# Sliding-window attention into a squared-ReLU MLP: two tiles loaded plainly, masks first, w_in ahead of w_out, global copies on VectorE, and the kT and xT evacuations on ScalarE

## Chip, cores, metric

One core of a Trainium2 chip. The metric is the device time of one execution in microseconds (us), the median of several. TensorE is called PE, VectorE DVE, ScalarE ACT, GpSimd POOL. An evacuation is a copy out of the PSUM tile into which PE has written; B4 is unit B of tile 4 (the units are explained below). "Cold" is PE at a lower granted clock. Profile line numbers (L189) belong to each kernel's own file, so one statement has different numbers before and after.

## The reference, cut

```python
# q, k, v: (4, 8, 768, 64) fp32; n_global = 8, n_local = 96
scores = q @ k.T / sqrt(64)
keep   = (column < 8) | (0 <= row - column < 96)
scores = where(keep, scores - slope[h] * dist, -1e9)   # ALiBi bias
attn   = softmax(scores) @ v                           # -> x (3072, 512)
out    = relu(x @ w_in) ** 2 @ w_out                   # w_in (512, 2048), w_out (2048, 512)
```

## The kernel before: what the argument touches

Attention is cut into 24 tiles of 128 rows, six a batch element, each in units A to F. The MLP is cut into 96 steps: 12 blocks of two tiles, by 8 slices of d_ff. "Stage 1" of a step makes hT, hr and hs; "stage 2" adds into acc and, at a block's end, copies acc out. A loop deals units between stages.

```python
def unit_a(j):                       # q and k of tile j transposed into ONE psum tile
    tr = ps_tr.tile([P, 2 * NPAIR, P], BF16, name="tr", tag="tr")    # bufs=1
    ... 4 transposes of q, 4 of k (PE) ...
    nc.vector.tensor_copy(z[:D, :, 0, :], tr[:D, :NPAIR, :])         # qz
    nc.vector.tensor_copy(z[D:, :, 1, :], tr[D:, :NPAIR, :])         # qz
    nc.vector.tensor_copy(kT[j], tr[:, NPAIR:, :])                   # kT

def globals_k(j):                    # after the scores of tile j
    nc.gpsimd.tensor_copy(kT[j][:, :, :n_global], g[:, :, :n_global])

# B, C (scores): matmuls into sc (bufs=1); esc = exp(sc) on ACT; at = esc * E on DVE
# D, E (values): matmuls into po (bufs=1); rs, x on DVE
# F: transposes of x into a tile of the same single "tr" buffer; xT copied out

def stage1(g):   # 8 matmuls -> hT (bufs=2); hr = relu(hT) on ACT; hs = hr*hr on DVE
def stage2(g):   # 4 matmuls -> acc (two psum tiles, bufs=1 each)
    if s == NSTEP - 1:               # block end
        for sub in range(2):
            nc.scalar.copy(o, acc[blk][sub])                         # frees acc
            nc.sync.dma_start(out=..., in_=o)

OFF = {"A": 0, "B": 1, "C": 2, "D": 3, "E": 4, "F": 6}   # steps; tile j at 4*(j-2)-4
...
for g in range(-1, NG + DELAY):      # DELAY = 2
    stage1(g); units due at g; load_tile every 4th step; stage2(g - DELAY)
```

Cut: loads (all from POOL's queue, casting fp32 to bf16), masks, shapes.

The softmax here doesn't subtract the row's maximum and nothing guards it: scores larger than these inputs give would overflow.

Of the kernel before, what the change touches and what calls it, by code (L numbers as in the profile page):

```python
# [12 lines left out]
FP32 = mybir.dt.float32  # L13
BF16 = mybir.dt.bfloat16
I32 = mybir.dt.int32
Act = mybir.ActivationFunctionType
Alu = mybir.AluOpType
# [4 lines left out]
def kernel(  # L22
# [11 lines left out]
    nc = tc.nc  # L34
    B, H, S, D = q.shape
    P = 128
    d_model, d_ff = moe_w_in.shape
    assert D == 64 and S % 256 == 0 and H == 8 and d_model == H * D
    TPB = S // P
    NT = B * TPB  # L40
    NPAIR = H // 2
    KM = d_model // P
    KF = d_ff // P
    n_global = int(n_global)
    n_local = int(n_local)
# [4 lines left out]
    slopes = [2.0 ** (-8.0 * (h + 1) / H) for h in range(H)]  # L50
    MASK_VAL = -1.0e6

    NSTEP = KF // 2
    NBLK = NT // 2

    consts = ctx.enter_context(tc.tile_pool(name="consts", bufs=1))
    work = ctx.enter_context(tc.tile_pool(name="work", bufs=2))
# [7 lines left out]
    def const(shape, dt, name):  # L65
        return consts.tile(shape, dt, name=name, tag=name)

    q_sb = [const([P, d_model], BF16, f"q_{j}") for j in range(NT)]
    k_sb = [const([P, d_model], BF16, f"k_{j}") for j in range(NT)]
    v_sb = [const([P, H, D + 1], BF16, f"v_{j}") for j in range(NT)]  # L70
    kT = [const([P, NPAIR, P], BF16, f"kT_{j}") for j in range(NT)]
    NQZ = 3
    qz = [const([P, NPAIR, 2, P], BF16, f"qz_{i}") for i in range(NQZ)]
    w_in_sb = [const([P, KM, 2 * P], BF16, f"win_{s}") for s in range(NSTEP)]
    w_out_sb = [const([P, 2, d_model], BF16, f"wout_{s}") for s in range(NSTEP)]
    ident = const([P, P], BF16, "ident")
    E = const([P, NPAIR, 2, 2, P], BF16, "E")
    E0 = const([P, NPAIR, 2, P], BF16, "E0")
    pb = const([P, 2, P], FP32, "pb")
    pb0 = const([P, P], FP32, "pb0")  # L80

    def load_tile(j):
        b, t = divmod(j, TPB)
        rows = slice(t * P, (t + 1) * P)
        for dst, src in ((q_sb[j], q), (k_sb[j], k)):
            nc.gpsimd.dma_start(  # L86
                out=dst.rearrange("p (h d) -> p h d", h=H),
                in_=src[b, :, rows, :].rearrange("h p d -> p h d"),
            )
        nc.gpsimd.dma_start(  # L90
            out=v_sb[j][:, :, :D], in_=v[b, :, rows, :].rearrange("h p d -> p h d")
        )

    def load_weights(s):
        f = slice(s * 2 * P, (s + 1) * 2 * P)
        nc.gpsimd.dma_start(
            out=w_in_sb[s], in_=moe_w_in[:, f].rearrange("(km p) f -> p km f", p=P)
        )
        nc.gpsimd.dma_start(
            out=w_out_sb[s], in_=moe_w_out[f, :].rearrange("(c p) m -> p c m", p=P)  # L100
        )


    for j in range(NT):
        nc.vector.memset(v_sb[j][:, :, D : D + 1], 1.0)
    load_tile(0)
    make_identity(nc, ident)
    for i in range(NQZ):
        nc.vector.memset(qz[i].bitcast(I32), 0)
    load_tile(1)  # L110

    for i, offset in enumerate((0, P)):
        dst = pb[:, i, :]
        nc.gpsimd.iota(
            dst.bitcast(I32), pattern=[[-1, P]], base=-offset, channel_multiplier=1
        )
        nc.gpsimd.tensor_copy(dst, dst.bitcast(I32))
        nc.gpsimd.affine_select(
            out=dst, in_=dst, compare_op=Alu.is_ge, fill=MASK_VAL,
            base=offset, pattern=[[1, P]], channel_multiplier=-1,  # L120
        )
        nc.gpsimd.affine_select(
            out=dst, in_=dst, compare_op=Alu.is_ge, fill=MASK_VAL,
            base=n_local - 1 - offset, pattern=[[-1, P]], channel_multiplier=1,
        )
    nc.gpsimd.tensor_copy(pb0, pb[:, 0, :])
    nc.gpsimd.tensor_scalar_max(
        pb0[:n_global, :], pb0[:n_global, :], float(-n_local)
    )
    nc.gpsimd.memset(pb[:n_global, 1, :], float(-n_local))  # L130
    for h in range(H):
        nc.scalar.activation(E0[:, h // 2, h % 2, :], pb0, Act.Exp, scale=float(slopes[h]))
    for h in range(H):
        nc.scalar.activation(E[:, h // 2, :, h % 2, :], pb, Act.Exp, scale=float(slopes[h]))

    for s in range(NSTEP):
        load_weights(s)
        if s % 2 == 1 and 2 + s // 2 < NT:
            load_tile(2 + s // 2)
    next_load = [2 + NSTEP // 2]  # L140


    attn = {}
    xT = {}

    def unit_a(j):
        tr = ps_tr.tile([P, 2 * NPAIR, P], BF16, name="tr", tag="tr")
        for pair in range(NPAIR):
            c = slice(pair * P, (pair + 1) * P)
            nc.tensor.transpose(out=tr[:, pair, :], in_=q_sb[j][:, c], identity=ident)  # L150
        for pair in range(NPAIR):
            c = slice(pair * P, (pair + 1) * P)
            nc.tensor.transpose(  # L153
                out=tr[:, NPAIR + pair, :], in_=k_sb[j][:, c], identity=ident
            )
        z = qz[j % NQZ]
        nc.vector.tensor_copy(z[:D, :, 0, :], tr[:D, :NPAIR, :])  # L157
        nc.vector.tensor_copy(z[D:, :, 1, :], tr[D:, :NPAIR, :])  # L158
        nc.vector.tensor_copy(kT[j], tr[:, NPAIR:, :])  # L159

    def globals_k(j):
        if 1 <= j % TPB < TPB - 1:
            g = kT[j - j % TPB]
            nc.gpsimd.tensor_copy(kT[j][:, :, :n_global], g[:, :, :n_global])  # L164

    def globals_v(j):
        if 1 <= j % TPB < TPB - 1:
            g = v_sb[j - j % TPB]
            nc.gpsimd.tensor_copy(v_sb[j][:n_global], g[:n_global])  # L169

    def unit_scores(j, hf):
        z = qz[j % NQZ]
# [38 lines left out]
        if first or hf == 1:  # L211
            globals_k(j)

    def unit_pv(j, hf):
# [36 lines left out]
        if hf == 1:  # L251
            globals_v(j)

    def unit_f(j):
        x = attn.pop((j, "x")).rearrange("p h d -> p (h d)")
        blk, tt = divmod(j, 2)
        if tt == 0:
            xT[blk] = work.tile([P, KM, 2 * P], BF16, name="xT", tag="xT")
        trx = ps_tr.tile([P, KM, P], BF16, name="trx", tag="tr")
        for kt in range(KM):  # L260
            nc.tensor.transpose(  # L261
                out=trx[:, kt, :], in_=x[:, kt * P : (kt + 1) * P], identity=ident
            )
        nc.vector.tensor_copy(xT[blk][:, :, tt * P : (tt + 1) * P], trx)

    UNITS = {
        "A": unit_a,
        "B": lambda j: unit_scores(j, 0),
        "C": lambda j: unit_scores(j, 1),
        "D": lambda j: unit_pv(j, 0),  # L270
        "E": lambda j: unit_pv(j, 1),
        "F": unit_f,
    }

# [4 lines left out]
    def stage1(g):  # L279
        blk, s = divmod(g, NSTEP)  # L280
        hT = ps_h.tile([P, 2, 2 * P], FP32, name="hT", tag="hT")
        for c in range(2):
            for kt in range(KM):
                nc.tensor.matmul(  # L284
                    out=hT[:, c, :],
                    lhsT=w_in_sb[s][:, kt, c * P : (c + 1) * P],
                    rhs=xT[blk][:, kt, :],
                    start=(kt == 0),
                    stop=(kt == KM - 1),
                    skip_group_check=True,  # L290
                )
        hr = work.tile([P, 2, 2 * P], FP32, name="hr", tag="hr")
        nc.scalar.activation(hr, hT, Act.Relu)  # L293
        hs = work.tile([P, 2, 2 * P], BF16, name="hs", tag="hs", bufs=4)
        nc.vector.tensor_mul(hs, hr, hr)  # L295
        hsq[g] = hs

    def stage2(g):
        blk, s = divmod(g, NSTEP)
        hs = hsq.pop(g)  # L300
# [20 lines left out]
                nc.sync.dma_start(out=out[r : r + P, :], in_=o)  # L321


    LEAD = 4
    OFF = {"A": 0, "B": 1, "C": 2, "D": 3, "E": 4, "F": 6}
    when = []
    for j in range(NT):
        for u, off in OFF.items():
            if u == "C" and j % TPB == 0:
                continue  # L330
            if j == 0:
                at_ = {"A": -100, "B": -98, "D": -96, "E": -95, "F": -93}[u]
            elif j == 1:
                at_ = {"A": -99, "B": -97, "C": -95.5, "D": -94, "E": -92, "F": -91}[u]
            else:
                at_ = 4 * (j - 2) - LEAD + off
            when.append((at_, j, u))
    when.sort()
    pos = 0
    DELAY = 2  # L340
    NG = NBLK * NSTEP
    for g in range(-1, NG + DELAY):
        if 0 <= g < NG:
            stage1(g)
        while pos < len(when) and when[pos][0] <= g:
            _, j, u = when[pos]
            UNITS[u](j)
            pos += 1
        if g >= 0 and g % 4 == 0 and next_load[0] < NT:
            load_tile(next_load[0])  # L350
            next_load[0] += 1
        if g - DELAY >= 0:
            stage2(g - DELAY)


# [1 line left out]
_INS = ['q', 'k', 'v', 'n_global', 'n_local', 'moe_w_in', 'moe_w_out']  # L357
_OUTS = [((3072, 512), 'float32')]
# [30 lines left out]
```

## Time and profile before

| | before |
|---|---|
| time, median of 3 | 281.2 us (280.94 to 281.26) |
| span in the profile | 279.3 us |
| PE busy / DVE / ACT / POOL | 81% / 58% / 42% / 33% |
| stage 1 of step 0 starts at | 42.65 us |
| two tiles in the body take | 20.3 us (2 x 10.13) |

PE has the most to do; what matters is where it stands still. The lines are in the prediction.

### The profile page before, as it was taken

What the parts mean: (1) busy time and instruction counts of PE and PEld (TensorE: products, weight loads), DVE (VectorE), ACT (ScalarE), POOL (GpSimd) and SP (SyncE); (2) the same over time, 40 slices, a digit from 0 to 9 for tenths busy, and PEclk for the clock granted to TensorE, in tenths of its full rate; (3) what the DMA queues carried; (4) which work ended last, traced back from release to release, by engine and by line L of the source; (5) the groups of instructions that cost most, each with busy time, mean ns of one, the idle gap of its engine ahead of it and who ended that gap; (6) DMA issues with size and microseconds to landing.
All of it is one profiled execution on the core that took longest, in us unless ns stands there. A gap on an engine that the chain in (4) does not pass through costs nothing.

```text
span 279.3 us, 4817 instructions
## 1 busy us (share of the span) xinstructions
PE 226.2 (81%) x1935; PEld 156.0 (56%) x1968; DVE 161.7 (58%) x359; ACT 117.4 (42%) x181; POOL 92.0 (33%) x137
## 2 busy tenths in 40 slices
PE   1335017988999898898999889889988988989994
PEld 0123015656666576576667557657666755766662
DVE  3335006766756766676675776766667577665441
ACT  1450013454446346346326435434453553453432
POOL 8987755227400413429000441365004000100000
PEclk9999999999999999999999999999999999999999
DMA  9999999698901449629902847859204610020102
GB/s 61 85 149 189 188 184 101 43 59 55 185 7 69 34 33 131 41 18 137 111 0 77 56 26 108 56 35 194 21 28 67 40 68 10 2 75 0 50 27 75
DMA packets 84757, 20.23 MB, mean 72 GB/s; under 512 B 75520, under 2 KB 81664, under 8 KB 84736
## 3 DMA queue, kind: packets, MB, share of 16 engines
q0 software_dynamic: 81280, 13.64, 63.4%
q1 hardware_dynamic: 3456, 6.29, 6.2%
q8 instruction: 15, 0.25, 0.4%
q14 instruction: 6, 0.05, 0.1%
HBM read 27.26 MB, written 6.29 MB: 120 GB/s over the span
## 4 chain that ended last, share of the span: by engine, by line
PE 59%; DVE 19%; POOL 6%; DMA 6%; ACT 5%; issue 3%; ACTq 0%; POOLq 0%
PE hT L284 24%; PE acc L308 23%; PE sc L189 7%; DVE hs L295 6%; ACT hr L293 5%; DVE kT L159 3%; DVE qz L158 3%; DVE x L245 3%; DMA win<-in_moe_w_in_dram 3%; DMA wout<-in_moe_w_out_dram 3%; DVE qz L157 2%; PE po L235 2%; PE trx L261 2%; POOL q L86 1%; POOL k L86 1%
## 5 line engine op out<-in xcount | busy, mean ns | idle before, releaser
L293 ACT ACTIVATE hr<-hT 128x512 f32<-128x512 f32 x96 | 57.6, 600 | 107.2 <-PE hT L284 107.2
L295 DVE TENSOR_TENSOR hs<-hr 128x512 bf16<-128x512 f32 x96 | 69.7, 726 | 55.5 <-ACT hr L293 54.7
L284 PE MATMUL hT<-xT,win 128*128 128x256 bf16 x768 | 100.4, 274 | 0.2
L308 PE MATMUL acc<-wout,hs 128*128 128x512 bf16 x351 | 92.9, 379 | 1.5
L284 PEld LDWEIGHTS <-win 128*128 128x128 bf16 x768 | 75.4, 98 | 28.8
L198 ACT ACTIVATE esc<-sc 128x1024 bf16<-128x1024 f32 x44 | 45.0, 1024 | 40.6 <-PE sc L189 38.4
L207 DVE TENSOR_TENSOR at<-esc,E 128x1024 bf16<-128x1024 bf16 x44 | 30.3, 689 | 45.2 <-ACT esc L198 44.8
L189 PE MATMUL sc<-qz,kT 128*128 128x256 bf16 x160 | 26.0, 287 | 33.9 <-DVE kT L159 15.8
L308 PEld LDWEIGHTS <-hs 128*128 128x128 bf16 x384 | 35.0, 98 | 24.2 <-DVE hs L295 0.2
L189 PEld LDWEIGHTS <-kT 128*128 128x128 bf16 x160 | 13.9, 101 | 41.7 <-DVE kT L159 22.0
L164 POOL COPY kT<-kT 128x32 bf16<-128x32 bf16 x16 | 3.4, 212 | 86.0 <-PE sc L189 86.0
L169 POOL COPY v<-v 8x520 bf16<-8x520 bf16 x16 | 10.3, 643 | 58.5 <-PE po L235 58.5
L86 POOL DMA_DIRECT2D q<-in_q_dram x24 | 21.7, 904 | 2.5 <-DMA wout<-in_moe_w_out_dram 1.7
L90 POOL DMA_DIRECT2D v<-in_v_dram x24 | 21.8, 909 | 0.5 <-issue 0.2
L86 POOL DMA_DIRECT2D k<-in_k_dram x24 | 21.6, 901 | 0.0
L245 DVE TENSOR_TENSOR x<-po,rs 128x256 bf16<-128x256 f32 x48 | 20.4, 424 | 1.6
L235 PE MATMUL po<-v,at 128*128 128x65 bf16 x320 | 17.1, 198 | 2.3 <-DVE x L245 2.3
L235 PEld LDWEIGHTS <-at 128*128 128x128 bf16 x320 | 13.9, 100 | 8.6 <-DVE x L245 8.0
L150 PE MATMUL tr<-ident,q 128*128 128x128 bf16 x96 | 9.9, 230 | 7.3 <-DMA q<-in_q_dram 6.8
L157 DVE COPY qz<-tr 64x512 bf16<-64x512 bf16 x24 | 9.8, 407 | 7.0 <-PE tr L153 7.0
L319 ACT COPY o<-acc 128x512 f32<-128x512 f32 x24 | 12.8, 591 | 1.6 <-PE acc L308 1.6
L153 PE MATMUL tr<-ident,k 128*128 128x128 bf16 x96 | 10.0, 230 | 1.3 <-DMA k<-in_k_dram 1.3
(32 smaller groups left out, 101.9 us busy)
## 6 DMA issues: line engine op xcount, KB each, us to landing
out_dram<-o SPq DMA_DIRECT2D x24, 256.0 KB, 2.3
q<-in_q_dram POOLq DMA_DIRECT2D x24, 128.0 KB, 3.6
k<-in_k_dram POOLq DMA_DIRECT2D x24, 128.0 KB, 4.5
v<-in_v_dram POOLq DMA_DIRECT2D x24, 128.0 KB, 5.0
win<-in_moe_w_in_dram POOLq DMA_DIRECT2D x8, 256.0 KB, 8.6
wout<-in_moe_w_out_dram POOLq DMA_DIRECT2D x8, 256.0 KB, 8.6
```

The source lines that it names most:

```text
L86: nc.gpsimd.dma_start(out=dst.rearrange("p (h d) -> p h d", h=H), in_=src[b, :, rows, :].rearrange("h p d -> p h d"),)
L90: nc.gpsimd.dma_start(out=v_sb[j][:, :, :D], in_=v[b, :, rows, :].rearrange("h p d -> p h d"))
L157: nc.vector.tensor_copy(z[:D, :, 0, :], tr[:D, :NPAIR, :])
L189: nc.tensor.matmul(out=sc[:, pi, i * 2 * P : (i + 1) * 2 * P], lhsT=kT[kj][:, pair, :], rhs=z[:, pair, :, :], start=True, stop=True, skip_ ...
L198: nc.scalar.activation(out=esc, in_=sc.rearrange("p a b -> p (a b)"), func=Act.Exp, scale=scale)
L207: nc.vector.tensor_mul(at, esc, bias)
L235: nc.tensor.matmul(out=po[:, hi, :], lhsT=a4[:, hi // 2, i, hi % 2, :], rhs=v_sb[kj][:, h, :], start=(i == 0), stop=(i == 1), skip_group_c ...
L245: nc.vector.tensor_tensor(out=x[:, 4 * hf : 4 * hf + 4, :], in0=po[:, :, :D], in1=rs.to_broadcast([P, 4, D]), op=Alu.mult,)
L284: nc.tensor.matmul(out=hT[:, c, :], lhsT=w_in_sb[s][:, kt, c * P : (c + 1) * P], rhs=xT[blk][:, kt, :], start=(kt == 0), stop=(kt == KM - ...
L293: nc.scalar.activation(hr, hT, Act.Relu)
L295: nc.vector.tensor_mul(hs, hr, hr)
L308: nc.tensor.matmul(out=acc[blk][sub], lhsT=hs[:, c, sub * P : (sub + 1) * P], rhs=w_out_sb[s][:, c, :], start=(s == 0 and c == 0), stop=(s ...
```

## The change

Its intent: start the MLP earlier (masks and two plain loads first, every w_in before any w_out, stage 2 eight steps behind stage 1 so that w_out isn't needed at once), take the global copies out of POOL's queue, relieve DVE by moving two evacuations to ACT, and put A two steps ahead of B. Core of the diff:

```diff
+    DELAY = 8                                  # was 2
+    # q, k of tiles 0 and 1: nc.sync.dma_start of fp32; cast in unit_a:
+        if j < NPLAIN:
+            nc.vector.tensor_copy(q_sb[j], plain["q", j])
+            nc.vector.tensor_copy(k_sb[j], plain["k", j])
-        nc.vector.tensor_copy(kT[j], tr[:, NPAIR:, :])
+        nc.scalar.copy(kT[j], tr[:, NPAIR:, :])
-            nc.gpsimd.tensor_copy(kT[j][:, :, :n_global], g[:, :, :n_global])
+            nc.vector.tensor_copy(kT[j][:, :, :n_global], g[:, :, :n_global])
-            nc.gpsimd.tensor_copy(v_sb[j][:n_global], g[:n_global])
+            nc.vector.tensor_copy(v_sb[j][:n_global], g[:n_global])
-        nc.vector.tensor_copy(xT[blk][:, :, tt * P : (tt + 1) * P], trx)
+        nc.scalar.copy(xT[blk][:, :, tt * P : (tt + 1) * P], trx)
...  loads: v0, v1, tiles 2 and 3, all w_in, then w_out with tiles 4 and 5 between
...  masks: one pass over 256 columns on POOL, ahead of all its loads
+    put(0, A=-9, B=-8.9, D=-8.6, E=-8.4, F=-8.3)
+    put(1, A=-8.8, B=-8.7, C=-8.5, D=-8.2, E=-8.1, F=-7.9)
+    put(2, A=-8.0, B=-7.8, C=0, D=1, E=2, F=3.3)
+    put(3, A=1.1, B=2.1, C=3, D=4, E=5, F=6)
+    put(4, A=10, B=11, C=11.5, D=12, E=13, F=14)
+    put(5, A=12.5, B=13.5, C=14.1, D=14.5, E=15, F=15.5)
+    put(6, A=15.2, B=16.5, C=17, D=18, E=19, F=20)
+    put(7, A=17.5, B=18.5, C=19.5, D=20.5, E=21.5, F=22.5)
+    for j in range(8, NT):
+        a0 = 4 * (j - 2) - 5
+        put(j, A=a0, B=a0 + 2, C=a0 + 3, D=a0 + 4, E=a0 + 5, F=a0 + 7)
```

(Also: hs has DELAY + 2 buffers, xT three, kT a ring of twelve; the loads of tiles 6 to 23 are all issued up front and no longer one every fourth step; a unit runs in the step that contains its number.)

More of the change, by code (lines that the diff above doesn't have):

```diff
@@ L70 @@
     v_sb = [const([P, H, D + 1], BF16, f"v_{j}") for j in range(NT)]
-    kT = [const([P, NPAIR, P], BF16, f"kT_{j}") for j in range(NT)]
+    NKT = 2 * TPB
+    kT_ring = [const([P, NPAIR, P], BF16, f"kT_{j}") for j in range(NKT)]
+    kT = [kT_ring[j % NKT] for j in range(NT)]
     NQZ = 3
@@ L80, with load_v @@
     pb0 = const([P, P], FP32, "pb0")
+    def load_v(j):
+        b, t = divmod(j, TPB)
+        nc.gpsimd.dma_start(
+            out=v_sb[j][:, :, :D],
+            in_=v[b, :, t * P : (t + 1) * P, :].rearrange("h p d -> p h d"),
+        )
     def load_tile(j):
@@ L89, in load_tile, with load_w_in @@
             )
-        nc.gpsimd.dma_start(
-            out=v_sb[j][:, :, :D], in_=v[b, :, rows, :].rearrange("h p d -> p h d")
-        )
-    def load_weights(s):
+        load_v(j)
+    def load_w_in(s):
         f = slice(s * 2 * P, (s + 1) * 2 * P)
@@ L98, in load_weights, with load_w_out @@
         )
+    def load_w_out(s):
+        f = slice(s * 2 * P, (s + 1) * 2 * P)
         nc.gpsimd.dma_start(
@@ L101, in load_weights @@
         )
-    for j in range(NT):
-        nc.vector.memset(v_sb[j][:, :, D : D + 1], 1.0)
-    load_tile(0)
+    NPLAIN = 2
+    plain = {}
+    for j in range(NPLAIN):
+        rows = slice(j * P, (j + 1) * P)
+        for n, src in (("q", q), ("k", k)):
+            t_ = const([P, d_model], FP32, f"plain_{n}{j}")
+            nc.sync.dma_start(
+                out=t_.rearrange("p (h d) -> p h d", h=H),
+                in_=src[0, :, rows, :].rearrange("h p d -> p h d"),
+            )
+            plain[n, j] = t_
     make_identity(nc, ident)
@@ L109 @@
         nc.vector.memset(qz[i].bitcast(I32), 0)
-    load_tile(1)
-    for i, offset in enumerate((0, P)):
-        dst = pb[:, i, :]
-        nc.gpsimd.iota(
-            dst.bitcast(I32), pattern=[[-1, P]], base=-offset, channel_multiplier=1
-        )
-        nc.gpsimd.tensor_copy(dst, dst.bitcast(I32))
-        nc.gpsimd.affine_select(
-            out=dst, in_=dst, compare_op=Alu.is_ge, fill=MASK_VAL,
-            base=offset, pattern=[[1, P]], channel_multiplier=-1,
-        )
-        nc.gpsimd.affine_select(
-            out=dst, in_=dst, compare_op=Alu.is_ge, fill=MASK_VAL,
-            base=n_local - 1 - offset, pattern=[[-1, P]], channel_multiplier=1,
-        )
-    nc.gpsimd.tensor_copy(pb0, pb[:, 0, :])
-    nc.gpsimd.tensor_scalar_max(
+    for j in range(NT):
+        nc.vector.memset(v_sb[j][:, :, D : D + 1], 1.0)
+    nc.gpsimd.iota(
+        pb.bitcast(I32), pattern=[[-P, 2], [-1, P]], base=0, channel_multiplier=1
+    )
+    nc.gpsimd.tensor_copy(pb, pb.bitcast(I32))
+    nc.gpsimd.affine_select(
+        out=pb, in_=pb, compare_op=Alu.is_ge, fill=MASK_VAL,
+        base=0, pattern=[[P, 2], [1, P]], channel_multiplier=-1,
+    )
+    nc.gpsimd.affine_select(
+        out=pb, in_=pb, compare_op=Alu.is_ge, fill=MASK_VAL,
+        base=n_local - 1, pattern=[[-P, 2], [-1, P]], channel_multiplier=1,
+    )
+    nc.vector.tensor_copy(pb0, pb[:, 0, :])
+    nc.vector.tensor_scalar_max(
         pb0[:n_global, :], pb0[:n_global, :], float(-n_local)
     )
-    nc.gpsimd.memset(pb[:n_global, 1, :], float(-n_local))
+    nc.vector.memset(pb[:n_global, 1, :], float(-n_local))
     for h in range(H):
@@ L134 @@
         nc.scalar.activation(E[:, h // 2, :, h % 2, :], pb, Act.Exp, scale=float(slopes[h]))
+    for j in range(NPLAIN):
+        load_v(j)
+    for j in range(NPLAIN, 4):
+        load_tile(j)
     for s in range(NSTEP):
-        load_weights(s)
-        if s % 2 == 1 and 2 + s // 2 < NT:
-            load_tile(2 + s // 2)
-    next_load = [2 + NSTEP // 2]
+        load_w_in(s)
+    for s in range(NSTEP):
+        load_w_out(s)
+        if s in (3, 5):
+            load_tile(4 + (s - 3) // 2)
+    for j in range(6, NT):
+        load_tile(j)
     attn = {}
@@ L257, in unit_f @@
         if tt == 0:
-            xT[blk] = work.tile([P, KM, 2 * P], BF16, name="xT", tag="xT")
+            xT[blk] = work.tile([P, KM, 2 * P], BF16, name="xT", tag="xT", bufs=3)
         trx = ps_tr.tile([P, KM, P], BF16, name="trx", tag="tr")
@@ L293, in stage1 @@
         nc.scalar.activation(hr, hT, Act.Relu)
-        hs = work.tile([P, 2, 2 * P], BF16, name="hs", tag="hs", bufs=4)
+        hs = work.tile([P, 2, 2 * P], BF16, name="hs", tag="hs", bufs=DELAY + 2)
         nc.vector.tensor_mul(hs, hr, hr)
@@ L321, in stage2, with put @@
                 nc.sync.dma_start(out=out[r : r + P, :], in_=o)
-    LEAD = 4
-    OFF = {"A": 0, "B": 1, "C": 2, "D": 3, "E": 4, "F": 6}
     when = []
-    for j in range(NT):
-        for u, off in OFF.items():
-            if u == "C" and j % TPB == 0:
-                continue
-            if j == 0:
-                at_ = {"A": -100, "B": -98, "D": -96, "E": -95, "F": -93}[u]
-            elif j == 1:
-                at_ = {"A": -99, "B": -97, "C": -95.5, "D": -94, "E": -92, "F": -91}[u]
-            else:
-                at_ = 4 * (j - 2) - LEAD + off
-            when.append((at_, j, u))
+    def put(j, **at_):
+        for u, t_ in at_.items():
+            if not (u == "C" and j % TPB == 0):
+                when.append((t_, j, u))
+    put(0, A=-9, B=-8.9, D=-8.6, E=-8.4, F=-8.3)
[9 more added lines that the diff above has]
+        put(j, A=a0, B=a0 + 2, C=a0 + 3, D=a0 + 4, E=a0 + 5, F=a0 + 7)
     when.sort()
     pos = 0
-    DELAY = 2
     NG = NBLK * NSTEP
@@ L344 @@
             stage1(g)
-        while pos < len(when) and when[pos][0] <= g:
+        while pos < len(when) and when[pos][0] < g + 1:
             _, j, u = when[pos]
@@ L348 @@
             pos += 1
-        if g >= 0 and g % 4 == 0 and next_load[0] < NT:
-            load_tile(next_load[0])
-            next_load[0] += 1
         if g - DELAY >= 0:
```

## The prediction

> **What bounds the kernel now.** I began with the page's busy times, then read the opening and one period of the body in order of time, and last the DMA rates.
>
> The kernel is a stream of 96 steps. Step g has a "stage 1" (8 matmuls against w_in into hT) and a "stage 2" (4 matmuls against w_out into acc). Units A to F of 24 attention tiles are dealt out between the steps. The page:
>
> ```profile
> span 279.3 us, 4817 instructions
> PE 226.2 (81%) x1935; PEld 156.0 (56%) x1968; DVE 161.7 (58%) x359; ACT 117.4 (42%) x181; POOL 92.0 (33%) x137
> ```
>
> PE is the bound, with 53 us in which it does nothing. The question is where those lie. The opening, in order of time:
>
> ```profile
> 5.00 0.60 PE L150 MATMUL tr<-ident,q 128*128 128x128 bf16 x4 [5.00 <-DMA q<-in_q_dram]
> 10.75 1.70 ACT L132 ACTIVATE E<-pb 128x128 bf16<-128x128 f32 x8 [8.73 <-POOL pb L127]
> 12.36 2.54 ACT L134 ACTIVATE E<-pb 128x256 bf16<-128x256 f32 x8
> 14.80 1.00 ACT L198 ACTIVATE esc<-sc 128x1024 bf16<-128x1024 f32 x1
> 24.53 0.42 DVE L264 COPY xT<-trx 128x512 bf16<-128x512 bf16 x1 [0.49 <-PE trx L261]
> 38.31 0.87 POOL L90 DMA_DIRECT2D v<-in_v_dram  x1 [0.18 <-issue]
> 39.18 0.22 POOL L164 COPY kT<-kT 128x32 bf16<-128x32 bf16 x1
> 39.45 0.56 PEld L189 LDWEIGHTS <-kT 128*128 128x128 bf16 x4 [11.94 <-POOL kT L164]
> 42.65 1.90 PE L284 MATMUL hT<-xT,win 128*128 128x256 bf16 x8
> ```
>
> Two delays stand here. Masks come after six DMA issues on POOL, so the first softmax starts at 14.80. Later the first block's xT is ready at 24.95, but PE stands still from 27.8 to 39.45, because a 0.22 us copy of global keys sits in POOL's queue behind every weight and tile issue, and POOL may issue only as the DMA drains. Stage 1 of step 0 starts at 42.65.
>
> The body, one period of four steps and one tile, in order of time:
>
> ```profile
> 113.48 0.29 PEld L235 LDWEIGHTS <-at 128*128 128x128 bf16 x8 [0.27 <-DVE x L245]
> 116.41 0.42 DVE L159 COPY kT<-tr 128x512 bf16<-128x512 bf16 x1
> 116.90 0.61 PE L189 MATMUL sc<-qz,kT 128*128 128x256 bf16 x4 [0.82 <-DVE kT L159]
> ```
>
> Unit B (scores) waits 0.82 us for the last of three evacuations on DVE, after A only one step earlier; E waits 0.27 for D's x. The chain and starts of hT (92.37, 102.49, 112.62) give a period of 10.13. Its parts, from start to start of PE groups where nothing waits: stage 1 0.87, stage 2 0.866; A 0.44, B 0.43, C 0.43, D 0.24, E 0.24, F 0.22, so 2.0 to 2.05 a tile. 4 x 1.733 + 2.05 = 8.98; the remaining 1.15 is those two waits. The list of waits from 60 to 270 us says the same over the body:
>
> ```profile
> PE sc L189 <- DVE kT L159: 12.4, 16, 0.8
> PEld L235 <- DVE x L245: 4.5, 17, 0.3
> ```
>
> Check by sum: 42.65 + 96 x 1.733 (166.4) + tile work still open (E, F of tile 2; 21 tiles; three of them lack C: 42.2) + 3.7 after the last matmul (275.6) = 255. The other 24.3 are 20 x 1.1, 0.85 for a cold first stage 1 (1.72 us on the chain, 0.87 later) and a wait of 1.2 at 47.7. So nothing else is hidden.
>
> DMA rates, in windows (last columns: DMA share, GB/s written):
>
> ```profile
> 8.00:10.00 2.00, 0.72 (x6) 0.46 (x7) 0.55 (x2) 0.00 (x0) 1.73 (x7) 1.00 1.87 119
> 32.00:34.00 2.00, 0.00 (x0) 0.00 (x0) 0.00 (x0) 0.00 (x0) 1.13 (x3) 1.00 1.39 201
> ```
>
> Tiles move at 97 to 122 GB/s (384 KB as bf16, about 3.4 us a tile), weights at 200 (256 KB in 1.3 us). Everything loaded early takes 10.4 x 2 + 13.6 = 34 us of the DMA from 12.3 on, so weights ended near 45.
>
> **What the Trainium skill says.** "DMA: Bandwidth & Descriptors", section "SWDGE vs HWDGE vs iDMA": only a load from GpSimd's queue can cast, and the hardware path of the sync queue is quicker to set up. This is why the plain loads need a cast on chip; here q landed 3.8 us after its issue at 1.24 by the cast path, and no plain load exists in this trace. "VectorE: DVE Perf Modes", "The perf-mode tier table": an fp32 copy within SBUF runs at 2x; with its 150 fixed cycles that makes (150 + 256)/0.96 GHz = 0.42 us per cast, an estimate from that page; no such copy is in the trace. "TensorE: Matmul & The Clock Gate", Part 1: the array starts at half clock after idleness; the 1.72 against 0.87 us agrees. "SBUF — State Buffer", "Who interferes with whom": DVE and GpSimd share a port pair; hs at 114.16 took 0.93 instead of 0.69 just while POOL copied v at 113.93, which agrees.
>
> **The change, part by part.** "Time" is from the span's start; each step comes from the durations above.
>
> *Masks first, plain q and k.* POOL needs about 2.9 us for identity and masks over 256 columns (0.4 to 0.5 each, scaled from 0.29 for 128). DVE's small fixes end near 3.7; E0 and E (1.7 + 2.54, 16 exponentials) then hold ACT until 8.0. The loads are no longer what waits: at 1.15 us per 128 KB of tile, q0 to k1 land from about 4 to 8.5. But kT now sits on ACT behind E: kT0 8.6, scores of tile 0 8.7 to 9.7, softmax 10.85.
>
> *The prologue as a chain.* DVE runs in program order, so the casts of tile 1 come after tile 0's multiplication (11.6): casts 12.3 to 12.4, transposes 13.0 (cold), qz 13.9, B1 14.9, softmax 16.0, D0's x 17.4, C1 17.1, its softmax 18.2 and product 18.95, x of E0 19.7, F0 20.2 and xT on ACT 20.85, D1 and E1 to x 22.4. A2 stands between E1 and F1 and both use the one transpose buffer, so F1 waits for qz of tile 2 (23.5); xT of F1 at 24.6. B2, cold, ends at 25. Stage 1 starts at 25.0, 17.6 earlier than before. The first w_in, behind 4 tiles (13.6 us from about 2), lands near 18.6 and the eighth near 28, so no weight is waited for.
>
> *Steps 0 to 7, stage 1 alone.* w_out isn't needed until step 8. PE has 8 x 0.87 + 0.85 cold + 2.25 + 0.44 of tiles 2 and 3, about 10.1; but short steps expose the latency of softmax, products and qz. Walking the queues: C2 26.75, B3 waits for qz3 until 31.75, C3 for the softmax 33.4, E3 for x 37.6, F3 39.0, step 8 at 40.1. So 15.1 us, 5 of them waits.
>
> *Steps 8 to 15.* Both stages and tiles 4 and 5: 13.9 + 4.55 of PE, plus C4 behind B4 in the same step (1.2), E5 behind C5 (1.2), F5 behind the evacuation of A6 (1.5), small ones 0.3: 22.6, step 16 at 62.7. Tile 4 lands near 36.5 for 44.4, tile 5 near 42.5 for 51, the last w_out near 45 for 61.8: DMA stays ahead.
>
> *Body.* B now comes two steps after A, so qz has 4.4 us of PE work to hide in where it needs 3.3; kT runs beside it on ACT. A stands between D and E, so PE has 2.4 us before E where x takes 2.4. Both waits should nearly vanish, 1.15 to 0.1. DVE gives away 10.2 + 9.9 us (kT, xT at 425 and 415 ns), and takes 16 x 2 small global copies, estimated 0.1 and 0.25: 6 us; ACT gains 48 x 0.6 (as o and hr, 128x512 from PSUM) = 29 us, and is then busy about 6.3 of 9 us a period. Neither binds. From step 16: 80 x 1.733 = 138.6, the eight stage 2 still owed 6.9, tile work 35.2, waits 2.0, end 3.7.
>
> Sum: 25.0 + 15.1 + 22.6 + 138.6 + 6.9 + 35.2 + 2.0 + 3.7 = 249.1 of span. The time of the kernel before is 1.9 above its span (281.2 against 279.3), so 251.0. The gain of 30: the start gives about 17.6 less the 9 us of waits added in steps 0 to 15 and some earlier tile work; the rest is 20 times the lost wait of 1.1.
>
> **Rivals.** (1) *ACT becomes the pacemaker*: hr, softmax, kT, xT and o in one in-order queue. Against it: 6.3 of 9 us; for it: where F and C meet, xT, the softmax and hr follow one another and delay hs, x and E. At 0.4 us a tile that is 7 us: 258. (2) *DMA ahead of PE*: if the 256-byte plain loads, or both queues together, run at two thirds of the tile rate, w_in comes 3 to 5 us later and w_out is met at step 12: 255. The present DMA share of 1.4 to 1.9 (saturated) speaks for tightness, the 5 us margins against. (3) *The short steps hide better than I walked them*, or the prologue is quicker: 245. (4) *The start is hidden anyway*, same total: would need PE idle elsewhere; 11.6 us behind POOL on the chain speak against, and the body would gain alone: 265.
>
> **Range and chances.** The body's 180 us are firm to about 4, the opening to about 5 either way: 244 to 258. Even without any gain in the body or with rival 4 it is over 2% faster.
>
> **What would show it.** Stage 1 of step 0 near 25 and step 16 near 63 in order of time; no wait of PE on POOL; B's waits for kT or qz gone in the body and a period of 9.0 to 9.1; xT and kT near 0.6 us on ACT; stage 1 not waiting on DMA. Wrong if the period stays above 9.5, if hT waits for hr, or if the first hT stands behind w_in or starts past 29.

## The result, and the profile after

269.36 us, median of 4 (268.28 to 269.87), against 281.07 (280.84 to 281.26) of the kernel before: ratio 0.9579, 95% interval 0.9547 to 0.961. Here and below a ratio is the mean time of one kernel's runs over that of the kernel before in the same rounds, so not quite the ratio of the medians quoted. Executions over 1.5% slower than the fastest of the same kernel are left out of the means. Faster, as predicted, but by 11.7 us and not by 30; 251.0 was predicted and 269.4 lies outside 244 to 258.

The page after (to be set against the first lines in the prediction):

```profile
span 266.5 us, 4844 instructions
PE 223.3 (84%) x1935; PEld 160.3 (60%) x1968; DVE 151.1 (57%) x350; ACT 139.8 (52%) x229; POOL 73.4 (28%) x94
```

DVE is busy 10.6 us less and ACT 22.4 us more (reckoned: about 14 less, 20 given away against 6 taken on, and 29 more). No engine is full, yet PE idles 43 us.

Milestones, beside the prediction's own (us from the span's start):

| | predicted | after | its length, predicted | its length, after |
|---|---|---|---|---|
| stage 1 of step 0 starts | 25.0 | 26.66 | 25.0 | 26.7 |
| stage 1 of step 8 starts | 40.1 | 42.54 | 15.1 | 15.9 |
| stage 1 of step 16 starts | 62.7 | 67.54 | 22.6 | 25.0 |
| end of span | 249.1 | 266.5 | 186.4 | 199.0 |

So 12.6 of the 17.4 us of error arise after step 16, 4.8 before. The end of a block in the body, in order of time, is where:

```profile
144.90 0.60 ACT L323 ACTIVATE hr<-hT 128x512 f32<-128x512 f32 x1 [0.40 <-PE hT L314]
146.34 0.42 DVE L275 TENSOR_TENSOR x<-po,rs 128x256 bf16<-128x256 f32 x1
146.68 0.41 DVE L187 COPY qz<-tr 64x512 bf16<-64x512 bf16 x1
147.10 0.43 DVE L188 COPY qz<-tr 64x512 bf16<-64x512 bf16 x1
147.62 0.58 ACT L189 COPY kT<-tr 128x512 bf16<-128x512 bf16 x1 [2.13 <-DVE qz L188]
148.10 1.08 ACT L349 COPY o<-acc 128x512 f32<-128x512 f32 x2
148.75 1.08 PE L338 MATMUL acc<-wout,hs 128*128 128x512 bf16 x4 [1.22 <-ACT o L349]
```

Read it from the bottom. PE waits 1.22 us for acc, which o has to empty. ACT does o right after kT, and before kT it stood 2.13 us although nothing else was running on it: kT began only when DVE's second qz copy ended. DVE came to qz only after hs and x. kT and qz read different halves of tr and write different tiles, so no data passes between them; they take turns all the same. The prediction had kT "beside" qz.

The list of waits (who waited for whom, us in total, times, longest) shows how often; eight of the nine waits on o are such block ends, of 1.22 to 1.45 us, and the ninth is 0.30 at the very end:

```profile
ACT kT L189 <- DVE qz L188: 45.1, 20, 3.5
PE acc L338 <- ACT o L349: 10.5, 9, 1.4
```

The waits that the change was to remove from the body did go: in the block above E (at 147.12) and B (at 150.54) show no wait. Two tiles take 149.67 - 130.28 = 19.39 us, or 9.7 a tile; 17.96 was predicted (two times 8.98, the prediction's sum without waits). Its own sign of being wrong, a period above 9.5, has come true.

The opening, in order of time:

```profile
24.76 0.58 ACT L189 COPY kT<-tr 128x512 bf16<-128x512 bf16 x1 [3.02 <-DVE qz L188]
25.40 0.59 PE L291 MATMUL trx<-ident,x 128*128 128x128 bf16 x4 [1.62 <-ACT kT L189]
26.66 1.89 PE L314 MATMUL hT<-xT,win 128*128 128x256 bf16 x8
```

The same turn-taking: F of tile 1 needs the transpose buffer, which kT of tile 2 leaves last of three copies in a row. It had struck before, at tile 1: there kT began at 14.31, behind qz, and the softmax ended at 17.04 where 16.0 was predicted.

### The profile page after: what moved, and what is told of

It is laid out like the page before. It is cut to its first block, busy times and chain, and to the rows that moved or that the text cites. A ratio compares the mean times of both kernels' runs of the same rounds, so it can differ in the third digit from the quotient of the medians.

```text
span 266.5 us, 4844 instructions
## 1 busy us (share of the span) xinstructions
PE 223.3 (84%) x1935; PEld 160.3 (60%) x1968; DVE 151.1 (57%) x350; ACT 139.8 (52%) x229; POOL 73.4 (28%) x94
## 4 chain that ended last, share of the span: by engine, by line
PE 66%; DVE 16%; ACT 11%; issue 5%; ACTq 0%
PE acc L338 27%; PE hT L314 26%; PE sc L219 7%; DVE hs L325 4%; ACT hr L323 4%; DVE x L275 3%; DVE qz L188 2%; ACT esc L228 2%; PE po L265 2%; ACT o L349 2%; PE trx L291 2%; DVE qz L187 2%; ACT kT L189 2%; DVE at L237 1%; DVE rs L274 1%
## 5 line engine op out<-in xcount | busy, mean ns | idle before, releaser
L325 DVE TENSOR_TENSOR hs<-hr 128x512 bf16<-128x512 f32 x96 | 66.3, 691 | 69.6 <-ACT hr L323 69.3
L338 PE MATMUL acc<-wout,hs 128*128 128x512 bf16 x351 | 92.9, 379 | 12.3 <-ACT o L349 10.5
L338 PEld LDWEIGHTS <-hs 128*128 128x128 bf16 x384 | 35.7, 98 | 37.6 <-issue 13.2
L189 ACT COPY kT<-tr 128x512 bf16<-128x512 bf16 x24 | 14.0, 584 | 50.8 <-DVE qz L188 45.1
L87 POOL DMA_DIRECT2D v<-in_v_dram x24 | 23.4, 975 | 2.6 <-DMA win<-in_moe_w_in_dram 1.2
L219 PEld LDWEIGHTS <-kT 128*128 128x128 bf16 x160 | 15.3, 102 | 10.6 <-ACT kT L189 6.1
L265 PEld LDWEIGHTS <-at 128*128 128x128 bf16 x320 | 15.1, 100 | 5.7 <-DVE x L275 4.9
L294 ACT COPY xT<-trx 128x512 bf16<-128x512 bf16 x24 | 14.0, 582 | 3.1 <-PE trx L291 3.1
L291 PE MATMUL trx<-ident,x 128*128 128x128 bf16 x96 | 9.9, 226 | 5.7 <-ACT kT L189 4.1
L291 PEld LDWEIGHTS <-x 128*128 128x128 bf16 x96 | 7.5, 100 | 6.9 <-issue 4.5
```

The source lines that it names most:

```text
L87: nc.gpsimd.dma_start(out=v_sb[j][:, :, :D], in_=v[b, :, t * P : (t + 1) * P, :].rearrange("h p d -> p h d"),)
L219: nc.tensor.matmul(out=sc[:, pi, i * 2 * P : (i + 1) * 2 * P], lhsT=kT[kj][:, pair, :], rhs=z[:, pair, :, :], start=True, stop=True, skip_ ...
L265: nc.tensor.matmul(out=po[:, hi, :], lhsT=a4[:, hi // 2, i, hi % 2, :], rhs=v_sb[kj][:, h, :], start=(i == 0), stop=(i == 1), skip_group_c ...
L291: nc.tensor.transpose(out=trx[:, kt, :], in_=x[:, kt * P : (kt + 1) * P], identity=ident)
L325: nc.vector.tensor_mul(hs, hr, hr)
L338: nc.tensor.matmul(out=acc[blk][sub], lhsT=hs[:, c, sub * P : (sub + 1) * P], rhs=w_out_sb[s][:, c, :], start=(s == 0 and c == 0), stop=(s ...
```

## The experiments

Twelve kernels ran, all gave a correct result. The kernel before ran beside each group on its chip: 280.69 beside the first four, 281.05 beside the next four, 280.88 beside the next three, 280.91 beside the last. Theory: **kT on ACT takes its turn behind qz, and ACT's in-order queue makes o, and so acc, wait**. Rivals: **ACT has too much work**; for the opening, **the DMA is the real bound**.

### 1. Stage 2 nine steps behind instead of eight

```diff
-    DELAY = 8
+    DELAY = 9
```

> The changed kernel with S2 nine steps behind S1 instead of eight; every instruction the same in kind and number. Theory (a queue accident: at every block end kT stands in ACT's queue waiting 2.1 us for qz on DVE, and the two o copies that free acc stand behind it): the block now ends in the step of unit E, where no kT stands ahead of o; the nine waits of acc on o (10.5 us in the changed kernel) fall below 1 us, two tiles take 18.0 to 18.2 us instead of 19.39, time 256 to 258 against 269.4. Rival (ACT has too much work, o is late wherever it stands): the waits stay within 2 us of 10.5 and the time is 268 to 270.

Measured: 257.78 us (ratio to before 0.9177). The block now ends in E's step. ACT, in order of time:

```profile
144.04 0.59 ACT L189 COPY kT<-tr 128x512 bf16<-128x512 bf16 x1 [2.13 <-DVE qz L188]
144.53 0.60 ACT L323 ACTIVATE hr<-hT 128x512 f32<-128x512 f32 x1
145.02 1.08 ACT L349 COPY o<-acc 128x512 f32<-128x512 f32 x2
```

kT still waits 2.13 us for qz, but o no longer follows it with PE waiting; the waits of acc on o come to 0.2 us, once. Two tiles take 158.19 - 140.25 = 17.94 us. ACT's work is the same in kind and number, so 11.6 us of the shortfall come from where o stands in its queue. "Too much work" falls. (All four runs have a clock of 0.990 to 0.993; in the profiled one it was 0.66 from 50 to 55 us.)

### 2. kT back on DVE

```diff
-        nc.scalar.copy(kT[j], tr[:, NPAIR:, :])
+        nc.vector.tensor_copy(kT[j], tr[:, NPAIR:, :])
```

> The changed kernel with only kT given back to DVE. Theory (kT on ACT waits behind qz and blocks ACT's queue): ACT no longer stands still there, the waits of acc on o nearly vanish, time 256 to 259. Its price, 24 times 0.42 us on DVE, shows only as a wait of some 0.1 to 0.4 us of B or E in some tiles. Rival (ACT has too much work): about half of the gain, since only one of the two moved copies is gone: 262 to 264. Second rival (B needs kT beside qz, so kT on ACT is what shortened the body): B waits for kT again about 0.4 to 0.8 us a tile, time 266 to 272.

Measured: 251.79 us (251.68 to 254.15), ratio 0.8991: 17.6 us faster than the changed kernel by the medians, more than expected. Stage 1 of body steps two tiles apart, in order of time:

```profile
141.27 1.04 PE L314 MATMUL hT<-xT,win 128*128 128x256 bf16 x8
159.22 1.04 PE L314 MATMUL hT<-xT,win 128*128 128x256 bf16 x8
```

17.95 us for two tiles. Milestones: step 0 at 25.25, step 8 at 40.09, step 16 at 63.92, span 249.9 (predicted 25.0, 40.1, 62.7, 249.1). With the one copy back on DVE the kernel does what the prediction said of the change. That doesn't bear out its walk through the opening, which had kT on ACT; there the agreement is in part luck. Of the 6.0 us gained over experiment 1, 4.4 are there by step 16 (63.92 against 68.30 there, which includes that cold spell). Against the changed kernel, whose profiled run had no cold spell, 3.6 are gained by step 16 (67.54 there): PE's waits on kT fall from 11.3 to 8.2 us. On ACT kT begins 0.09 us after qz has ended and takes 0.58, on DVE it follows at once and takes 0.42. That these 0.25 us at the end of each row of three copies make up the whole difference is argued, not shown.

### 3. xT back on DVE, kT left on ACT

```diff
-        nc.scalar.copy(xT[blk][:, :, tt * P : (tt + 1) * P], trx)
+        nc.vector.tensor_copy(xT[blk][:, :, tt * P : (tt + 1) * P], trx)
```

> The changed kernel with only xT given back to DVE. Theory (the order kT before o, not the load of ACT): the body's nine waits of acc on o stay at 1.2 us each, time 267 to 271. Rival (ACT has too much work): as with kT given back, 257 to 264, and the waits of acc on o halve.

Measured: 270.01 us (0.9615), as the theory had it. ACT is relieved of as many instructions as in experiment 2 and nothing improves; from its list of waits:

```profile
ACT kT L189 <- DVE qz L188: 46.8, 20, 5.4
PE acc L338 <- ACT o L349: 10.2, 9, 1.4
```

### 4. The kernel before with only the global copies on DVE

```diff
-            nc.gpsimd.tensor_copy(kT[j][:, :, :n_global], g[:, :, :n_global])
+            nc.vector.tensor_copy(kT[j][:, :, :n_global], g[:, :, :n_global])
-            nc.gpsimd.tensor_copy(v_sb[j][:n_global], g[:n_global])
+            nc.vector.tensor_copy(v_sb[j][:n_global], g[:n_global])
```

> The kernel before with only the two small copies of global keys and values moved from POOL to DVE. If the wait of 11.6 us on POOL was the opening's real bound: stage 1 of step 0 starts at 30 to 32 instead of 42.65 and most of it is kept, time 269 to 272 against 281.1, so this one line would be worth as much as the whole change. Rival (DMA is the bound just behind: weights and tiles 4 and 5 end near 45 whatever POOL does): stage 1 or 2 then waits for win, wout or q of tiles 3 to 5, and 3 to 6 us are left of it, time 275 to 278. The body's waits on kT (0.82 us a tile) stay in both.

Measured: 269.61 us (0.9606), as fast as the whole change. Step 0, in order of time:

```profile
30.44 0.64 PE L235 MATMUL po<-v,at 128*128 128x65 bf16 x8
30.89 1.90 PE L284 MATMUL hT<-xT,win 128*128 128x256 bf16 x8
```

Stage 1 starts at 30.89 instead of 42.65, and nearly all of these 11.8 us is kept (the span is 11.6 shorter): PE waits neither for weights nor for tiles afterwards. The DMA was not the bound just behind. A by-product: the mean of hs on DVE falls from 726 to 692 ns by this edit alone, which agrees with the port that DVE and POOL share, as the prediction has it.

### 5. kT on ACT, but issued ahead of qz

```diff
+        nc.scalar.copy(kT[j], tr[:, NPAIR:, :])
         nc.vector.tensor_copy(z[:D, :, 0, :], tr[:D, :NPAIR, :])
         nc.vector.tensor_copy(z[D:, :, 1, :], tr[D:, :NPAIR, :])
-        nc.scalar.copy(kT[j], tr[:, NPAIR:, :])
```

> The changed kernel with one line moved: kT's copy on ACT is issued ahead of the two qz copies on DVE instead of behind them. Theory (the two engines take turns at the transpose tile[...], in program order, though neither writes it): the wait turns round, DVE's qz now waits for kT, ACT no longer stands 2.1 us for DVE, and the waits of acc on o vanish, so the body is as with kT on DVE; the opening gains nothing or loses 1 to 2 us (qz0 behind kT0, which is behind E). Time 253 to 257. Rival (no turn-taking; kT was late for a reason of its own): qz does not wait for kT, and acc still waits for o: 267 to 271.

Measured: 252.45 us (0.8982), a shade better than expected. The wait has turned round; first from the list of waits, then one of the four in order of time, from the opening:

```profile
DVE qz L188 <- ACT kT L187: 5.0, 4, 2.7
```

```profile
8.09 0.56 ACT L187 COPY kT<-tr 128x512 bf16<-128x512 bf16 x1
8.68 0.42 DVE L188 COPY qz<-tr 64x512 bf16<-64x512 bf16 x1 [2.69 <-ACT kT L187]
```

Neither copy writes what the other reads, and yet whichever is issued second waits for the first. That is the turn-taking, shown. In the body it now costs nothing, because DVE reaches qz later than ACT finishes kT:

```profile
146.17 0.59 ACT L187 COPY kT<-tr 128x512 bf16<-128x512 bf16 x1
147.27 0.41 DVE L188 COPY qz<-tr 64x512 bf16<-64x512 bf16 x1
```

Here acc waits for o 0.3 us, once. Two tiles take 159.96 - 142.01 = 17.95 us. The opening is 1.4 us behind that of experiment 2 (step 16 at 65.35).

### 6. The kernel before with A one step earlier

```diff
-    OFF = {"A": 0, "B": 1, "C": 2, "D": 3, "E": 4, "F": 6}
+    OFF = {"A": -1, "B": 1, "C": 2, "D": 3, "E": 4, "F": 6}
```

> The kernel before with only unit A issued one step earlier, so that B comes two steps behind it and A stands between D and E. By the prediction's step for the body both waits (B on kT 0.82, E on x 0.27) vanish in 20 tiles: 22 us at most; the start stays at 42 to 44. Time 259 to 264. Rival (the body's waits were tied to DVE's load, which here stays): 268 to 278.

Measured: 258.36 us (0.9186): 22.7 us from one number, a little more than expected. The group of score matmuls (count | busy us, mean ns | idle us before them, by releaser) had 15.8 us of waits on kT before; now:

```profile
L189 PE MATMUL sc<-qz,kT 128*128 128x256 bf16 x160 | 25.9, 286 | 20.3 <-POOL kT L164 12.2 <-ACT esc L198 6.7 <-DVE kT L159 1.4
```

1.4 us is left, with DVE's load unchanged. The single long wait on POOL stays, as it should.

### 7. Experiments 4 and 6 together

> The kernel before with the globals on DVE and unit A one step earlier, nothing else. If the two gains are independent: 11.1 from the globals and about 19 from the body, time 248 to 253, as fast as the changed kernel with kT on DVE; then plain loads, masks first, weights in two groups and the delay of eight add nothing net. Rival (with the body denser PE meets the DMA in steps 4 to 8): waits for wout or q, 254 to 259.

Measured: 246.22 us (0.8755), two us better than expected and 23.1 better than the changed kernel. 11.1 + 22.7 = 33.8 would be the sum of the single gains; 34.8 is measured. Its page:

```profile
span 244.0 us, 4855 instructions
PE 220.8 (90%) x1968; PEld 159.6 (65%) x1968; DVE 164.5 (67%) x391; ACT 115.0 (47%) x181; POOL 78.8 (32%) x105
```

The two edits that the change contains beside everything else are worth more than the change. Even with kT mended (251.8) it is 5.6 us slower than this, although its stage 1 starts at 25.25 and this one's at 31.73. Experiments 8, 10 and 12 look for that.

### 8. The change with kT on DVE, and three units of tiles 4 to 6 moved

```diff
-    put(4, A=10, B=11, C=11.5, D=12, E=13, F=14)
+    put(4, A=9, B=11, C=12, D=12.1, E=13, F=14)
-    put(6, A=15.2, B=16.5, ...)
+    put(6, A=15.6, B=16.5, ...)
```

> The changed kernel with kT on DVE and three units moved: A of tile 4 a step earlier, C and D of tile 4 half a step later, A of tile 6 behind F of tile 5. The waits in steps 8 to 16 (B4 0.44, C4 1.11, F5 1.58, which becomes about 0.8) shrink by about 2.3 us. Time 249 to 250.5 against 251.8. Rival (the chain of tile 5 to xT sets step 16 anyhow): 251 to 252.5.

Measured: 252.01 us (251.04 to 252.57, ratio 0.8952), no gain over experiment 2 that is clear of noise (ratio 0.8991, intervals overlap), as its rival had it: a miss. Some waits went (B4's, C4's), others grew or came (B5 from 0.50 to 0.78, A6 0.67), and then a cold spell: the granted clock is 0.66 from 60 to 65 us, and four stage 2 matmuls take

```profile
62.31 1.91 PE L338 MATMUL acc<-wout,hs 128*128 128x512 bf16 x4
```

instead of 1.03 us. Three of its four runs have a mean granted clock of 0.991; the one at 0.997 took 251.04. These three moves of single units didn't pay.

### 9. A version from what had paid so far

Plain loads, masks first and globals on DVE from the change; kT and xT on DVE; DELAY 2; w_in and w_out loaded in pairs with tiles between; and the body's order from the first step on:

```diff
+    put(0, A=-100, B=-98, D=-96, E=-95, F=-93)
+    put(1, A=-99, B=-97, C=-95.5, D=-94, E=-92, F=-91)
+    for j in range(2, NT):
+        a0 = 4 * (j - 2) - 5
+        put(j, A=a0, B=a0 + 2, C=a0 + 3, D=a0 + 4, E=a0 + 5, F=a0 + 7)
```

> A version made of what the runs so far paid for: plain loads of two tiles, masks first and globals on DVE from the change; kT and xT on DVE, S2 two steps behind S1 and w_in and w_out in pairs as before; A two steps ahead of B from the first step on. The first softmax should start near 9.5 instead of 14.8 and stage 1 of step 0 near 26.5 instead of 31.7 in the kernel before with globals on DVE and early A (246.2); the body stays free of waits: time 240 to 243. Rival (started 5 us earlier, PE runs into the DMA: win, wout or q of tiles 4 and 5 late in steps 5 to 9): 244 to 248.

Measured: 242.07 us (241.74 to 242.83), ratio 0.8616 [0.8592, 0.864]. The first softmax starts at 10.47, a microsecond later than expected; stage 1 of step 0 starts at 27.42 instead of 31.73 in experiment 7, and about 4 us of it are kept; PE has no wait for a weight or a later tile. It beats both kernels.

### 10. The change with kT on DVE and stage 2 two steps behind

```diff
-    DELAY = 8
+    DELAY = 2
```

> The changed kernel with kT on DVE and S2 two steps behind S1 instead of eight; loads and units in the order of the change. If the waits in steps 0 to 7 (about 4.5 us) are there because steps without S2 give PE nothing to do while softmax, products and qz run, they fill up: 246 to 249 against 251.8. Rival (w_out is really late, which is why S2 was put eight steps back): PE waits for wout in steps 2 to 9, 251 to 256.

Measured: 250.43 us (249.09 to 251.58), 1.4 us better than experiment 2 and between what was expected and its rival. The two ran on different chips, and the intervals of their ratios just touch (0.8908 [0.8864, 0.8952] against 0.8991 [0.8951, 0.9032]), so the gain is barely clear of noise. PE never waits for wout, so the delay of eight protected against nothing that shows here. Filling steps 0 to 7 took PE to the same waits in steps 10 to 15 as before; two of them, in order of time:

```profile
63.99 0.41 PE L265 MATMUL po<-v,at 128*128 128x65 bf16 x8 [0.73 <-DVE x L275]
66.42 0.40 PE L291 MATMUL trx<-ident,x 128*128 128x128 bf16 x4 [1.57 <-DVE kT L189]
```

### 11. Experiment 9 without the plain loads

```diff
-    NPLAIN = 2
+    NPLAIN = 0
+    load_tile(0)          # casting load ahead of the masks; tile 1 right behind them
```

> The first kernel of this batch without the plain loads: tile 0 by a casting load ahead of identity and masks, tile 1 right behind the masks. If masks first is what starts the softmax early and the plain loads only add to it: first softmax 11 to 12, 1.5 to 3 us slower than with plain loads, 242 to 245. Rival (both give the same, since E holds ACT until then): within 0.7 us of it. Second rival (the plain loads are all of it): as slow as 246.

Measured: 244.61 us (0.8706), 2.5 us more than with them, as expected; but the first softmax starts at 13.33 and not at 11 to 12. The masks now stand behind three load issues on POOL, so E starts at 9.27 instead of 4.03. So of the 4 us the plain loads give 2.5, by leaving POOL's queue to the masks as much as by landing early; the rest, some 1.5, goes with masks first and the order of loads. Useful, and small.

### 12. Experiment 10 with the even order of units

The put lines of experiment 9 in the kernel of experiment 10; loads (all w_in first) and xT on ACT stay as in the change.

> The changed kernel with kT on DVE and S2 two steps behind (250.4), and its units of tiles 0 to 7 in the even order of four steps a tile that the best version has (242.1); the loads stay in the order of the change (all of w_in ahead of w_out) and xT stays on ACT. If the change's own order of units in steps 0 to 24 is what still costs: 242 to 245, with at most a short wait for q of tile 4. Rival (the order of loads or xT is what costs): 247 to 251, with waits of PE for wout or q, or for xT.

Measured: 242.28 us (242.23 to 243.21), ratio 0.8632: 8.1 us better than experiment 10, level with experiment 9. From step 0 on PE shows no wait for a load or for xT (before it one of 0.67 us for xT). Step 0, in order of time:

```profile
28.04 1.56 PE L314 MATMUL hT<-xT,win 128*128 128x256 bf16 x8
```

It starts stage 1 2.7 us later than experiment 10 (25.38) and ends 7.3 us sooner in the profiled runs: with A always two steps ahead of B, each unit at least a step from the next, and A to D of tile 2 ahead of step 0, PE shows no wait at all from step 0 through step 24. The order of the weight loads and xT's engine make no difference that these runs show.

## Why the prediction was wrong, point by point

The ledger, by medians: 269.4 -> 251.8 (kT on DVE, -17.6) -> 250.4 (stage 2 two steps behind, -1.4) -> 242.3 (even order of units, -8.1).

- **The failed step.** "kT runs beside it on ACT" (body), and with it "1.15 to 0.1". The old waits did vanish, but kT does not run beside qz: it takes its turn after it (20 waits, 45.1 us of ACT) and hands the delay on to o and acc: 1.22 to 1.45 us of PE at eight block ends, 10.5 in all with the end, in a stretch from step 16 on that came out 12.6 us too long. Experiments 1, 2 and 5 take this away in three ways, and the body falls to the predicted 17.96 us for two tiles (17.94, 17.95 and 17.95).
- **Why it was missed.** The prediction summed ACT's work (6.3 of 9 us) and found room. It never walked ACT's queue at a block end, nor asked what else reads the tile that kT is copied from. The Trainium skill says it: "PSUM — Partial Sum Buffer", section "PSUM bank collisions raise a hardware error", tells that two engines may not access one bank in one partition at a time, reads included, and that the compiler's scheduler adds a dependency between ACT and DVE there. By that page's specifications a bank is 2 KiB a partition; tr, 8 x 128 bf16, is just that. The 2.13 us, and its turning round in experiment 5, agree; that it is the bank, and not the shared tile, is not shown (see below). The prediction cited four pages, and not the one on which the moved copy depended.
- **Rival 1 was near, for the wrong reason.** It gave ACT's queue 7 us through the meeting of F and C. The place was A and the block end, and load was not it (experiment 3).
- **The opening: sizes.** Step 0 came 1.7 us late, step 16 a further 3.2. Experiment 2 is nearly on the predicted milestones, so most of this is kT again: in A1, where B waits for it, and in A2 and A6, where F waits for the transpose buffer. (One sum of the prediction is off: the PE work of steps 0 to 7, 8 x 0.87 + 0.85 + 2.25 + 0.44, is 10.5 and not 10.1. Nothing rests on it; the 15.1 came from the walk.)
- **Right.** The wait on POOL was worth its 11 us (experiment 4); A two steps ahead removes the body's waits (22.7 in experiment 6, of which the prediction's working gives 20 x 1.1); the DMA stays ahead of PE (rival 2 falls); rival 4 falls, since experiment 4 keeps its earlier start; rival 3 falls too, since steps 0 to 15 took 40.9 us and not less than 37.7. The tail of the sum, 186.4 us from step 16, is 186.0 in experiment 2.
- **What the total hid.** The prediction noted 9 us of waits added in steps 0 to 15 and let them pass as the price of starting early. Experiments 7 and 12 show that the price need not be paid.

Left open: whether the turn-taking belongs to the PSUM bank or to the tile tr, which fills it (no kernel put the transposes of q and of k into two tiles); how much of the run-to-run spread of the kernels with many short pauses (the change: 268.28 at a mean clock of 1.000, 269.14 to 269.87 at 0.994) could be had back by the order of units; and what held some of the casts back (below).

## What to carry to other kernels

Before an evacuation is moved to a second engine, look at what the first engine still reads from the same PSUM tile: here the two took turns in issue order, and the in-order queue passed that wait on to what stood behind, the copy that frees the accumulator. Issue the copy of the engine that is free first, or let one engine do both. And price a change wait by wait: two small edits held 34.8 of 281 us, while a start 16 us earlier, bought with an uneven order of units, gave part of it back.

## What the Trainium skill lacked or had wrong

- "PSUM — Partial Sum Buffer" has the rule on bank collisions, but not its cost through the queues: 45.1 us of ACT in 20 waits, and 10.5 us of PE waiting for acc. "ScalarE: Activation LUTs" names a plain copy as work for ACT; it has no pointer to that rule.
- "VectorE: DVE Perf Modes" led to an estimate of 0.42 us for the fp32 to bf16 cast of 128x512 in SBUF. Of the two casts each of q and k in the changed kernel, those of q took 0.43 and 0.49 us, those of k 0.88 and 0.82. It isn't the shape, nor k: in experiment 8 the first cast of k took 0.43. In all nine kernels with plain loads that cast ends 0.26 to 0.29 us after POOL has begun its next load issue, wherever it began (5.09 to 5.55 us). So it was held until POOL's issue under way was nearly over, which would fit the port that DVE and POOL share; no run separates this.
- "DMA: Bandwidth & Descriptors" calls the hardware path quicker to first byte. No run shows a first byte. To landing the plain loads (256 KB each as fp32) took 3.9 us (q) and 4.3 us (k), the casting loads of the kernel before 3.6 and 4.5 (128 KB as bf16): not sooner, as far as unequal loads compare.
- "TensorE: Matmul & The Clock Gate" has half clock after idleness, and in experiment 8 four stage 2 matmuls took 1.91 instead of 1.03 us after pauses. Its table has the fall after an idle window of about 3.4 us; here no single pause before it was over 0.73 us, and pauses of 0.73 and 1.58 us at the same place in experiment 2 left the clock at 1.00. What tips it, no run shows.
